# Blocks 2 and 3 of a two-layer feed-forward kernel: y by seven products after all of h, weight jobs at other ticks, some sums on GpSimd

## The chip, the cores and the metric

One core of a Trainium2 chip. The time is the device time of one execution in microseconds (us). A profiled execution also leaves a span, from its first to its last instruction, and a trace of every engine: PE (TensorE matmuls), PEld (TensorE weight loads), DVE (VectorE), ACT (ScalarE), POOL (GpSimd) and SP (SyncE, which here issues all DMAs, in order).

## The reference

Attention over chunks of 32 tokens, then two feed-forward layers, all in float32. 4 x 768 tokens, 8 heads of 64, so the layers see x of 3072 x 512; their hidden width is 2048.

```python
for c in range(nc):                       # 24 chunks of 32 tokens per sequence
    k_full = concat([mem_k, k[16 before .. 8 after the chunk]])   # 8 memory keys, windows of 56
    scores = scale * q_c @ k_full.T
    a = softmax(scores)                   # over 64 keys
    out[chunk] = a @ v_full
...
h = x @ w_in                              # first layer
g = np.maximum(h, 0.0) + np.log1p(np.exp(-np.abs(h)))     # softplus
x = g @ w_out
...
h = x @ w_in                              # second layer, other weights
g = h - np.tanh(h)
return g @ w_out
```

The weights and activations reach TensorE as pairs of a high part (rounded to the engine's float32r) and a low part (the rest), and each product is three matmuls: high x high, high x low, low x high.

## The kernel before

**Blocks.** The 3072 tokens are six blocks of 512 (N). In the first layer, block j takes 16 row blocks of h (f = 0 to 15), each 4 x 3 = 12 matmuls of 128x128 by 512 (`ff_h`), and for y 16 x 4 x 3 = 192 matmuls (`ff_y1`). Blocks 0 to 3 run f by f: h of f, softplus into t, gh and gl (the two parts) on ScalarE and VectorE, and two steps later (LAG) y of f. Blocks 4 and 5 are done as one block of 1024: first all h (384 matmuls; `act_g` puts softplus straight into the g tiles), then y by seven products of half-size matrices instead of eight (`y_phase`, 7 x 8 x 6 = 336 matmuls). The second layer does both h and y by seven products, for three blocks of 1024 (`h_phase`, `y_phase`).

**What seven products need.** The second factor of each product is a sum or difference of quarters. For the weights these are made on the chip: `job_w1(p)` (first layer, w_out), `job_w(kind, p)` (second layer, both matrices, which also converts float64 words to float32), each ending in `split_to`: hi on ScalarE, its store, lo on VectorE, its store, to DRAM (`wod`, `wid`). For x of the second layer `job_x` does so. For g, `y_steps` makes the differences (t2 and two sums in place) and, three steps ahead of TensorE (AHEAD), gh and gl of the next product; `gh` and `gl` have three tiles each. Weights for products come back from DRAM through a ring of slots (`Ring`), those of h of blocks 4 and 5 through `t_load` from `w1id`.

**The order.** Every engine's order is written out by hand. After an opening (block 0 and the first eight of 24 attention units), `tick()` is called once per twelve matmuls of 128x512 and places the other work of that moment: DMAs put off by `defer`, then the attention unit of the moment (128 tokens: scores `s_mm`, softmax, transposes `t_mm`, the copy pT `t_out`, `v_mm`, the two parts of x `x_out`), one unit every six ticks, then one step of each running job, then softplus, gh and gl of the f at hand. `JOBS` lists the ticks at which jobs begin; a job issues its load, waits four ticks (LEAD), and goes on by a step per tick. Ticks 0 to 95 are blocks 1 to 3, 96 to 129 the h stage of blocks 4 and 5 with the last y steps of block 3, 130 to 157 their y stage, then 56 per block of the second layer.

**Tiles that several users share.** `o` (four tiles of 4 KB per partition, handed out in turn) serves hi and lo of the jobs, the outputs of a block (`out1`) and of a y stage; the next user of a tile waits until its store has landed. `c2` is a job's scratch, `w15` its raw input (`w6`, `w5` for the four jobs in SECOND).

```python
def split_to(src, dst, shape):
    hi = opool.tile([P, *shape], F32R, name="o")
    nc.scalar.copy(out=hi, in_=src)
    yield
    put(hi, dst(0))
    lo = opool.tile([P, *shape], F32R, name="o")
    nc.vector.tensor_tensor(out=lo, in0=src, in1=hi.bitcast(F32), op=ALU.subtract)
    defer(put, lo, dst(1))
```

## Time and profile before

| | before |
|---|---|
| median of 3 runs | 1057.54 us (1057.13 to 1058.17) |
| profiled execution, its own time | 1057.51 us |
| its span | 1055.4 us |
| granted TensorE clock, mean | 0.997 |
| busy PE / PEld / DVE / ACT / POOL | 99 / 81 / 69 / 54 / 1% of the span |
| DMA moved | 303.19 MB, 287 GB/s mean |

Busy shares are of the span. Matmuls are pipelined and their ends are modelled, so one matmul's duration (390 ns) is longer than the time from one to the next. In rows of the timeline the columns are start (us), duration (us), engine, line, operation, output<-inputs, count, and in brackets how long the engine was idle before and for whom. In rows of groups they are busy us and mean ns of one, then idle time before.

### The profile page before, as it was taken

What the parts mean: (1) busy time and instruction counts of PE and PEld (TensorE: products, weight loads), DVE (VectorE), ACT (ScalarE), POOL (GpSimd) and SP (SyncE); (2) the same over time, 40 slices, a digit from 0 to 9 for tenths busy, and PEclk for the clock granted to TensorE, in tenths of its full rate; (3) what the DMA queues carried; (4) which work ended last, traced back from release to release, by engine and by line L of the source; (5) the groups of instructions that cost most, each with busy time, mean ns of one, the idle gap of its engine ahead of it and who ended that gap; (6) DMA issues with size and microseconds to landing.
All of it is one profiled execution on the core that took longest, in us unless ns stands there. A gap on an engine that the chain in (4) does not pass through costs nothing.

```text
span 1055.4 us, 18458 instructions
## 1 busy us (share of the span) xinstructions
PE 1044.2 (99%) x7368; PEld 857.4 (81%) x7370; DVE 727.6 (69%) x1129; ACT 567.1 (54%) x904; POOL 7.8 (1%) x14
## 2 busy tenths in 40 slices
PE   7999999999999999999999999999999999999998
PEld 5787888888888888888888888888888888888886
DVE  6998445845755657487677687777487877446876
ACT  6996454645656455354454555544455554344553
POOL 2000000000000000000000000000000000000000
PEclk8999999999999999999999999999999999999999
DMA  9989945857777986999987999978799788656651
GB/s 377 407 327 358 337 171 186 301 187 236 263 248 248 312 307 195 341 361 352 325 326 281 359 371 347 341 294 320 272 363 347 293 321 305 224 170 213 243 202 61
DMA packets 101269, 303.19 MB, mean 287 GB/s; under 512 B 8000, under 2 KB 55104, under 8 KB 83520
## 3 DMA queue, kind: packets, MB, share of 16 engines
q1 hardware_dynamic: 101184, 302.02, 79.5%
q8 instruction: 58, 0.95, 0.4%
q14 instruction: 27, 0.22, 0.1%
HBM read 211.29 MB, written 90.70 MB: 286 GB/s over the span
## 4 chain that ended last, share of the span: by engine, by line
PE 97%; DVE 1%; ACT 1%; DMA 0%; issue 0%; ACTq 0%
PE ps_y L387 47%; PE ps_h L387 32%; PE ps_b L387 13%; PE ps_a L361 2%; PE ps_a L280 1%; PE ps_a L332 1%; PE ps_h L880 1%; DMA qk<-in_qk 0%; PE ps_yy L361 0%; PE ps_h L399 0%; DVE gl L427 0%; DVE t L307 0%; DVE x L327 0%; ACT o L170 0%; PE ps_a L268 0%
## 5 line engine op out<-in xcount | busy, mean ns | idle before, releaser
L387 PE MATMUL ps_h<-x,w 128*128 128x512 f32 x900 | 215.3, 390 | 0.1
L704 ACT CAST gh<-w 128x512 fp32r<-128x512 f32 x224 | 139.0, 622 | 140.3 <-DVE gl L645 120.2
L645 DVE TENSOR_TENSOR gl<-w,gh 128x512 fp32r<-128x512 f32 x236 | 163.0, 691 | 71.4 <-ACT gh L704 64.9
L387 PEld LDWEIGHTS ps_h<-x,w 128*128 128x128 f32 x900 | 168.6, 188 | 35.4 <-ACT t L410 0.2
L387 PE MATMUL ps_y<-gh,w 128*128 128x512 f32 x512 | 172.9, 399 | 0.0
L387 PEld LDWEIGHTS ps_y<-gh,w 128*128 128x128 f32 x512 | 96.1, 188 | 21.3
L387 PE MATMUL ps_y<-gh,x 128*128 128x512 f32 x352 | 109.4, 389 | 0.0
L387 PE MATMUL ps_y<-gl,w 128*128 128x512 f32 x256 | 99.7, 390 | 0.0
L387 PE MATMUL ps_y<-w,x 128*128 128x512 f32 x402 | 94.5, 389 | 0.0
L387 PEld LDWEIGHTS ps_y<-w,x 128*128 128x128 f32 x402 | 75.5, 188 | 15.7
L427 DVE TENSOR_TENSOR gl<-t,gh 128x512 fp32r<-128x512 f32 x64 | 45.5, 713 | 55.8 <-ACT gh L422 55.6
L668 ACT ACTIVATE tanh<-sum 128x512 f32<-128x512 f32 x72 | 45.5, 632 | 60.0 <-DVE sum L641 59.8
L387 PEld LDWEIGHTS ps_y<-gh,x 128*128 128x128 f32 x352 | 66.1, 188 | 13.7
L410 ACT ACTIVATE t<-ps_h 128x512 f32<-128x512 f32 x64 | 38.1, 598 | 69.4 <-PE ps_h L387 65.8
L387 PE MATMUL ps_b<-gh,x 128*128 128x512 f32 x176 | 68.5, 389 | 0.0
L387 PE MATMUL ps_h<-gh,x 128*128 128x512 f32 x176 | 68.5, 389 | 0.0
L387 PE MATMUL ps_y<-gl,x 128*128 128x512 f32 x176 | 68.5, 389 | 0.0
L448 ACT CAST o<-c 128x1024 fp32r<-128x1024 f32 (+1 forms) x32 | 31.0, 969 | 69.6 <-DVE c L493 41.1
L645 DVE TENSOR_TENSOR w<-w 128x512 f32<-128x512 f32 x88 | 60.5, 688 | 6.8 <-ACT w L410 5.8
L387 PEld LDWEIGHTS ps_y<-gl,w 128*128 128x128 f32 x256 | 48.2, 188 | 9.0
L387 PE MATMUL ps_y<-x,w 128*128 128x512 f32 x240 | 55.2, 389 | 0.0
L387 PE MATMUL ps_b<-w,x 128*128 128x512 f32 x216 | 54.8, 389 | 0.0
(160 smaller groups left out, 1611.6 us busy)
## 6 DMA issues: line engine op xcount, KB each, us to landing
x<-wod SPq DMA_DIRECT2D x44, 1024.0 KB, 4.7
w<-x2d SPq DMA_DIRECT2D x21, 1024.0 KB, 6.8
x<-wid SPq DMA_DIRECT2D x21, 1024.0 KB, 6.1
wod<-o SPq DMA_DIRECT2D x32, 512.0 KB, 6.1
qk<-in_qk SPq DMA_DIRECT2D x21, 768.0 KB, 6.5
x2d<-o SPq DMA_DIRECT2D x30, 512.0 KB, 7.2
x<-wid SPq DMA_DIRECT2D x18, 768.0 KB, 6.8
ring<-wod SPq DMA_DIRECT2D x12, 1024.0 KB, 5.3
```

Of the source, the lines that this page charges most:

```text
L280: nc.tensor.matmul(out=ps[cc, j, KEYS * p : KEYS * (p + 1)], lhsT=a["q"][r, p, cc], rhs=a["k"][r, c, p, :], start=True, stop=True,)
L332: nc.tensor.transpose(ps[:, p * P : (p + 1) * P], a["sm"][:, p * P : (p + 1) * P], ident)
L361: nc.tensor.matmul(out=ps[h : h + 64, p % 2, 2 * P + t0 : 2 * P + t0 + CHUNK], lhsT=v, rhs=pT, start=True, stop=True,)
L387: nc.tensor.matmul(out=ps, lhsT=a, rhs=b, start=first and i == 0, stop=last and i == 2, skip_group_check=on,)
L410: nc.scalar.activation(out=out, in_=x, func=AF.Softplus)
L427: eng.tensor_tensor(out=gl, in0=t, in1=gh.bitcast(F32), op=ALU.subtract)
L448: nc.scalar.copy(out=hi, in_=src)
L645: nc.vector.tensor_tensor(out=out, in0=x, in1=y, op=ALU.subtract)
L668: nc.scalar.activation(out=t, in_=h, func=AF.Tanh)
L704: nc.scalar.copy(out=gh, in_=src)
L880: nc.tensor.matmul(out=ps_h[1], lhsT=zeros[:, :P], rhs=zeros, start=True, stop=True)
```

## The change

In blocks 2 and 3, which were two plain blocks, first all h is computed (`h_step`: f upward for block 2, downward for block 3, softplus into g tiles), then y of both by seven products (`y_phase(0, ...)`), as blocks 4 and 5 had it. Their w_in comes through `t_load` from `w1id` into w0 to w6 (`T1_LOADS`), the y weights through a ring of five of these slots. So w_out's sums (`job_w1`) must be ready by tick 66: all eight now begin at ticks 3 to 28, and their scratch c is an `o` tile. The t2 differences are made in the h stage, after each softplus of block 3 with f below 8. The attention units come at the ticks of `ATT_AT`, in plain order; x of units 20 to 22 no longer goes by way of DRAM (`x1d`); units 10, 11, 21 and 22 have their exponentials on ScalarE as eight instructions (`LATE_ACT`). Nine of the 16 w2 jobs (`BY_ACT`) convert with three ScalarE instructions and one of VectorE instead of one and three. Jobs whose sums fall into ticks 105 to 120 do these on GpSimd, and put the two halves of their sums through gh and gl tiles instead of o tiles. The x jobs of the first pair of blocks begin at ticks 86 and 94 (before: 42 and 54). Now ticks 0 to 31 are block 1, 32 to 65 h of blocks 2 and 3, 66 to 93 their y, 94 to 125 h of blocks 4 and 5, 126 to 153 their y; the second layer is as before.

```diff
-ATT_STEP = 6
-ATT_ORDER = (8, 9, 10, 11, 20, 12, 13, 14, 15, 21, 16, 17, 18, 19, 22, 23)
-VIA_DRAM = (20, 21, 22)
+ATT_AT = (0, 6, 14, 20, 28, 33, 38, 42, 46, 50, 54, 59, 64, 68, 74, 86, 92)
+ATT_FROM = 2 * UB
...
+T1_SLOT = (0, 4, 3, 2, 1, 5, 6, 0)
+T1_RING = (1, 2, 3, 4, 0)
+W1_ORDER = (7, 0, 4, 3, 2, 1, 5, 6)
 JOBS = (
-    (1, 15, 24, 43, 53, 76, 85, 94),
-    (5, 14, 23, 33, 66, 75, 84, 92, 95, 99, 102, 106, 109, 113, 117, 152),
-    (42, 54, 159, 169, 214, 224),
+    (3, 8, 4, 11, 18, 22, 25, 28, ),
+    (8, 15, 27, 37, 43, 49, 55, 89, 96, 99, 102, 105, 108, 111, 131, 148, ),
+    (86, 94, 156, 169, 206, 220, ),
 )
-SECOND = (95, 102, 109, 117)
-PHASES = ((1, NT - 1),) + tuple((2, b) for b in range(NT))
+SECOND = (89, 96, 102, 108, )
+BY_ACT = (8, 15, 27, 55, 99, 108, 111, 131, 148, )
+X_SLOT = (15, 7, 15, 15, 15, 15, )
+T1_LOADS = {9: 0, 13: 1, 17: 2, 21: 3, 25: 4, 29: 5, 33: 6, 38: 7, 54: 0}
+LATE_ACT = (10, 11, 21, 22, )
+T2_H = (105, 121)
+PHASES = ((1, 1), (1, 2)) + tuple((2, b) for b in range(NT))
...
+    def split_halves(src, dst):
+        for s in range(2):
+            ts = []
+            for i in (0, 2):
+                t = gpool.tile([P, 2, HALF], F32R, name="gl" if s else "gh")
+                if s:
+                    nc.vector.tensor_tensor(
+                        out=t, in0=src[:, i : i + 2], in1=his[i // 2].bitcast(F32), op=ALU.subtract
+                    )
+                else:
+                    nc.scalar.copy(out=t, in_=src[:, i : i + 2])
+                ts.append(t)
...
+        if by_act:
+            x = pool.tile([P, 4 * HALF, 2], U16, name=name, bufs=1)
+            nc.scalar.mul(x[:, :, 1].bitcast(F16), hi.bitcast(F32), SIGN_ONLY)
+            nc.scalar.activation(
+                out=x[:, :, 0], in_=lo, func=AF.Identity, scale=LOW_SCALE, bias=low_bias
+            )
+            nc.scalar.mul(hi.bitcast(F32), hi.bitcast(F32), EXP_BIAS)
+            yield
+            c = x.rearrange("p n two -> p (n two)").bitcast(U32)
             nc.vector.scalar_tensor_tensor(
-                out=c, in0=of, scalar=k, in1=c, op0=op, op1=ALU.bitwise_or
+                out=c, in0=hi, scalar=3, in1=c, op0=ALU.logical_shift_left, op1=ALU.bitwise_or
             )
...
-        sums(w)
-        yield
-        yield from split_to(w, lambda s: ((0, 4, place(s, 2, 4)),), [4, HALF])
-
-    def sums(w):
+        far = T2_H[0] <= now[0] < T2_H[1]
+        sums(w, nc.gpsimd if far else nc.vector)
+        yield
+        if far:
+            yield
+        if T2_H[0] <= now[0] < T2_H[1]:
+            yield from split_halves(w, lambda s, i: place(s, 2 + i, 2))
+        else:
+            yield from split_to(w, lambda s: ((0, 4, place(s, 2, 4)),), [4, HALF])
...
-        nc.vector.tensor_tensor(out=w[:, 2], in0=w[:, 2], in1=w[:, 1], op=sub)
-        nc.vector.tensor_tensor(out=w[:, 3], in0=w[:, 3], in1=w[:, 1], op=sub)
+        eng = eng or nc.vector
+        eng.tensor_tensor(out=w[:, 0], in0=w[:, 0], in1=w[:, 3], op=add)
+        eng.tensor_tensor(out=w[:, 1], in0=w[:, 0], in1=w[:, 1], op=sub)
+        eng.tensor_tensor(
+            out=w[:, 2:4], in0=w[:, 2:4], in1=w[:, 1:2].to_broadcast([P, 2, HALF]), op=sub
+        )
...
     def job_w1(p):
-        c = tpool.tile([P, 4, HALF], F32, name="c2", bufs=1)
+        c = opool.tile([P, 4, HALF], F32, name="o")
...
+                if not b and p % 4 == 3 and i * 2 + p // 4 >= 9:
+                    s = i * 2 + p // 4 - 9
+                    defer(t_load, s, s)
...
+        steps = [(0, f) for f in range(NF)] + [(1, f) for f in reversed(range(NF))]
+        prepared = []
+        t2 = []
+        prep = y_steps(prepared, t2)
+        ring = Ring((0,), ())
+        for n, (t, f) in enumerate(steps):
+            if t and f == NP - 1:
+                t2.extend(t2_tiles())
+            h_step(n, n == len(steps) - 1, t, f, x_tile(2 + t), t and f < NP and t2)
             if pend:
                 run_y()
                 tick()
+            if t and f % 2 == 0 and f < 2 * T_RING:
+                s = T1_RING[T_RING - 1 - f // 2]
+                defer(lambda s=s: ring.add(wpool.tile([P, 2048], F32R, name=f"w{s}")))
+        y_phase(0, prep, prepared)
```

`h_step` is the body of the old loop over h of blocks 4 and 5 (`ff_h`, then a tick with `act_g`), made a function; `act_g` gained one line:

```diff
+            if t2:
+                minus(t2[f // 4][:, f % 4], g2[f][:, 3], g)
```

## Rows read from the trace of the kernel before

**Rows 1.** The page: busy us of the engines, and the main DMA queue.
```profile
PE 1044.2 (99%) x7368; PEld 857.4 (81%) x7370; DVE 727.6 (69%) x1129; ACT 567.1 (54%) x904; POOL 7.8 (1%) x14
q1 hardware_dynamic: 101184, 302.02, 79.5%
```
**Rows 2.** Waits of PEld from 127 us on: total us, times, longest us.
```profile
PEld ps_a L361 <- issue: 4.6, 13, 0.4
```
**Rows 3.** The chain that ended last: start us, us, what.
```profile
670.75 76.16 PE ps_y L387 x336
```
**Rows 4.** Windows: length, busy us by engine (count), clock, DMA share, GB/s.
```profile
186.46:205.37 18.91, 18.91 (x205) 15.57 (x205) 17.31 (x30) 11.58 (x16) 0.00 (x0) 1.00 0.87 295
...
429.00:518.40 89.40, 89.40 (x396) 74.00 (x395) 61.60 (x86) 40.23 (x59) 0.00 (x0) 1.00 0.95 335
...
594.60:670.75 76.15, 76.15 (x337) 63.05 (x337) 59.35 (x94) 44.20 (x76) 0.00 (x0) 1.00 0.96 350
```
**Rows 5.** Groups by line and form: gl, softplus, pT.
```profile
L645 DVE TENSOR_TENSOR gl<-w,gh 128x512 fp32r<-128x512 f32 x236 | 163.0, 691 | 71.4 <-ACT gh L704 64.9
...
L410 ACT ACTIVATE t<-ps_h 128x512 f32<-128x512 f32 x64 | 38.1, 598 | 69.4 <-PE ps_h L387 65.8 <-DVE gl L427 2.9 <-PE ps_y L387 0.4
...
L344 ACT COPY pT<-ps_a 128x512 f32<-128x512 f32 x20 | 11.6, 582 | 3.9 <-PE ps_a L332 3.9
```
**Rows 6.** Timeline, ticks 1 to 6.
```profile
128.72 1.35 DVE L513 TENSOR_TENSOR c<-w 128x256 f32<-128x256 f32 x3
...
131.82 1.06 ACT L448 CAST o<-c 128x1024 fp32r<-128x1024 f32 x1 [2.63 <-DVE c L493]
...
135.95 3.69 SPq L788 DMA_DIRECT2D y1d<-o  x4
...
139.72 1.23 DVE L452 TENSOR_TENSOR o<-c,o 128x1024 fp32r<-128x1024 f32 x1 [0.42 <-DMA y1d<-o]
...
143.76 1.14 PE L361 MATMUL ps_a<-pT,v 64*64 64x32 f32 x64
```
**Rows 7.** DMA issues: count, KB each, median us to landing.
```profile
wod<-o SPq DMA_DIRECT2D x32, 512.0 KB, 6.1
...
y1d<-o SPq DMA_DIRECT2D x24, 256.0 KB, 7.1
```
**Rows 8.** Timeline after the scores of one unit.
```profile
145.72 0.59 ACT L375 CAST x<-ps_a 128x512 fp32r<-128x512 f32 x1 [0.60 <-PE ps_a L280]
...
146.34 0.69 DVE L307 TENSOR_REDUCE st<-ps_a 128x8 f32<-128x512 f32 x1 [4.79 <-ACT x L375]
...
147.67 0.68 DVE L377 TENSOR_TENSOR x<-ps_a,x 128x512 fp32r<-128x512 f32 x1
```
**Rows 9.** Timeline in the y stage of blocks 4 and 5.
```profile
551.11 0.62 ACT L704 CAST gh<-w 128x512 fp32r<-128x512 f32 x1 [0.74 <-DVE gl L645]
551.76 0.69 DVE L645 TENSOR_TENSOR gl<-w,gh 128x512 fp32r<-128x512 f32 x1
553.85 0.39 PE L387 MATMUL ps_b<-gl,x 128*128 128x512 f32 x1
```
**Rows 10.** Timeline: exponentials of one unit of the opening, first and last of 16.
```profile
84.33 1.28 ACT L316 ACT_TABLE_LOAD   x1
85.63 0.31 ACT L316 ACTIVATE sm<-ps_a,st 128x64 f32<-128x64 f32 x1
...
87.86 0.24 ACT L316 ACTIVATION_READ_ACCUMULATOR sm<-ps_a,st 128x1 f32 x1
```
**Rows 11.** Groups by line and form: GpSimd's subtractions in the opening.
```profile
L198 POOL TENSOR_TENSOR w<-o,w 128x1024 fp32r<-128x1024 f32 x1 | 2.4, 2399 | 72.5 <-ACT w L196 72.5
...
L198 POOL TENSOR_TENSOR w<-o,w 128x512 fp32r<-128x512 f32 x1 | 1.7, 1662 | 18.7 <-ACT w L196 18.7
```
**Rows 12.** Window in the h stage of blocks 4 and 5, columns as in rows 4.
```profile
450.00:490.00 40.00, 40.00 (x178) 33.10 (x178) 31.20 (x44) 18.23 (x27) 0.00 (x0) 1.00 1.01 356
```

More of the change, by code (lines that the diff above doesn't have):

```diff
@@ L1 @@
+from bisect import bisect_right
 from contextlib import ExitStack
@@ L75 @@
 SHARED = (7, 15)
-PLAIN = NB - 2
 T_LAG = 3
@@ L516, in job_w1, with job_x @@
         yield from split_to(c, lambda s: ((0, 4, wod[0][:, 2:6, p, s]),), [4, HALF])
-    def job_x(b, e, second=False):
-        raw = wpool.tile([P, 2, 2, N], F32, name="w6" if second else "w15")
+    def job_x(b, e, slot):
+        raw = wpool.tile([P, 2, 2, N], F32, name=f"w{slot}")
         nc.sync.dma_start(out=raw, in_=y1d[b][e])
@@ L693, in h_phase, with t2_tiles, y_steps @@
                 tick()
-    def y_steps(prepared):
-        t2 = [wpool.tile([P, 4, N], F32, name=f"w{i}") for i in (5, 6)]
-        sums_left = [(n, p) for n in range(3) for p in range(NP)]
+    def t2_tiles():
+        return [wpool.tile([P, 4, N], F32, name=f"w{i}") for i in (5, 6)]
+    def y_steps(prepared, t2=None):
+        sums_left = [(n, p) for n in range(0 if t2 is None else 1, 3) for p in range(NP)]
+        t2 = t2_tiles() if t2 is None else t2
         for q in PRODUCTS:
@@ L741, in y_phase @@
         for i, q in enumerate(PRODUCTS):
-            ps = [banks[(2 * b + d) % 4][i % 2] for d in range(2)]
+            ps = [(banks[2 * (b - 1) + d & 3] if b else ps_y[2 * d : 2 * d + 2])[i % 2] for d in range(2)]
             for p in range(NP):
@@ L800, in tick @@
                 run(soft.pop(u))
-        if r == 1 and before in VIA_DRAM:
-            run(soft.pop(("x", before)))
+        if k in T1_LOADS:
+            t_load(T1_LOADS[k], T1_SLOT[T1_LOADS[k]])
         active.extend(job() for job in plan.get(k, ()))
@@ L810, in tick @@
             s_mm(u, ps_a)
-        if r == 4 and u is not None:
+        t = min(4, ATT_AT[i + 1] - ATT_AT[i] - 1) if u is not None else -1
+        if r == t:
             t_mm(u, ps_a[:, 0, :])
         next(chain, None)
-        if r == 4 and u is not None:
+        if r == t:
             t_out(u)
@@ L959, in attention_ffn_ffn @@
             g = g2[f % NP][:, 2 * (f // NP) + t]
-            if n == len(steps) - 1:
-                prepared = []
-                prep = y_steps(prepared)
+            if last:
                 for _ in range(AHEAD):
                     next(prep)
-            tick(act_g(g, ps, g2[f][:, 0] if t and f < NP else None))
+            step()
+            tick(act_g(g, ps, g2[f][:, 0] if t and f < NP else None, f, t2))
+        steps = [(0, f) for f in range(NF)] + [(1, f) for f in reversed(range(NF))]
[7 more added lines that the diff above has]
+            h_step(n, n == len(steps) - 1, t, f, x_tile(2 + t), t and f < NP and t2)
             if pend:
@@ L968, in attention_ffn_ffn @@
                 tick()
[L969 to L975 removed]
+            if t and f % 2 == 0 and f < 2 * T_RING:
+                s = T1_RING[T_RING - 1 - f // 2]
+                defer(lambda s=s: ring.add(wpool.tile([P, 2048], F32R, name=f"w{s}")))
+        y_phase(0, prep, prepared)
+        steps = []
+        for f in range(NF + T_LAG):
+            steps += [(0, f)] * (f < NF) + [(1, f - T_LAG)] * (f >= T_LAG)
+        prepared = []
+        prep = y_steps(prepared)
+        for n, (t, f) in enumerate(steps):
+            x = x_tile(2 * (NT - 1) + t)
+            h_step(n, n == len(steps) - 1, t, f, x)
+            if now[0] > ATT_AT[-1] + 1 and lpool is None:
                 attention.close()
```

172 lines of the change are left out of this document (82 added, 90 removed).

## The prediction

> **What bounds the kernel now.** I read the profile from the engines inward. Shares first: TensorE is busy for 99% of the span; the DMA queue's packets take 79.5% of 16 engines [rows 1]. Then the waits of TensorE and of its weight loads from 127 us on, after the opening: for the matmuls the view lists none, for the loads gaps of at most 0.4 us [rows 2]. So from there the span is the sum of TensorE's work. Its rate: 336 matmuls in 76.16 us, 226.7 ns each [rows 3]; twelve of them, one tick of the planner, take 2.72 us. An edit pays if it takes matmuls away, and costs what it makes TensorE wait. The stages come last [rows 4]: the granted clock is 1.00, the 2.4 GHz level, in all of them; in the h stage of blocks 4 and 5 (429 to 518 us) VectorE works 61.6 of 89.4 us and DMA stands at 0.95, in the next h stage at 0.96.
>
> **The gain is a count.** Each of blocks 2 and 3 takes 192 matmuls for y; seven products take 7 x 8 x 6 = 336 for both. Their h stays at 384, the attention units stay at 16. 48 matmuls x 226.7 ns = **10.9 us**, four ticks: y of blocks 4 and 5 now begins with tick 126 instead of 130. All else is a question of waits. I walked the new order of instructions along TensorE's timeline with the durations of rows: gl 0.69, softplus 0.60, pT 0.58 us [rows 5].
>
> **Ticks 0 to 32 (block 1): eight w1 jobs and three w2 jobs.** A w1 job now takes its scratch c from the four o tiles. At tick 3 these hold the outputs of block 0, and c of the first job must wait until the first of them is stored: in before a lo of VectorE waited for the same release, to 139.72 us [rows 6]. c takes 3.1 us (128.72 to 131.82), so it is ready at 142.8. The planner puts hi of this job on ScalarE at tick 4, ahead of softplus and pT of unit 8: 1.06 + 0.60 + 0.58, less small overlaps, gives pT at 144.9. V of unit 8 wants it at 143.76 [rows 6]. A stall of **1.2 us**. The second job, a tick later, needs an o tile whose store has just gone out (median 6.1 us [rows 7]), so VectorE stands until 150 us; the softmax of unit 9 then ends near 156, its transposes are due at 158: covered by 2 us. Further on I find none in the block: a softplus result has 8 us until its bank is wanted. The w1id loads issued here have 10 to 20 ticks before use.
>
> **Ticks 32 to 66 (h of blocks 2 and 3).** The units come every four or five ticks. Between transposes and V of a unit lie 2.72 us; softplus and pT need 1.2, so 1 to 2 us are spare. At tick 35 hi of the w2 job begun at 27 takes an o tile that block 1's outputs have just filled, and waits for that store: 3.7 us (135.95 to the release [rows 6]) to 7.1 (the median [rows 7]). Softplus and pT of unit 13 stand behind: 0 to 1.7 us, I take **0.8**. Around tick 59 the job with three conversions on ScalarE and the differences t2 on VectorE push the job's sums until hi of tick 63 stands ahead of pT of unit 19: 0 to 1.4, I take **0.7**.
>
> **The step to y, tick 66.** Unit 20 is scored at tick 64, one h step before y begins. What follows a unit's scores (there they ended at 145.6): xh on ScalarE, then maximum, subtraction and xl on VectorE [rows 8]. After these stand two differences of the h step, and only then the first gl: 0.7 + 6 x 0.67 = 4.7 us after the scores, where the matmul that reads it is due at 2.72 + 0.23 = 2.95. A stall of 1.9 us; the last softplus, with a table load before the exponentials and one after, delays the softmax of unit 20 by some 0.4 more: **2.3 us**. Before, the step into a y stage had no attention unit and no differences beside it, since f ran upward there.
>
> **Ticks 66 to 94 (y of blocks 2 and 3).** The rhythm of a y stage: gh starts when its tile comes free (551.11), gl ends at 552.45, the matmul that wants it starts at 553.85 [rows 9]: 1.4 us of cover. Units 21 and 22 have their exponentials on ScalarE as eight instructions; such a group takes 2.5 us (85.63 to 88.10), after a table load of 1.28 [rows 10]. For unit 21 the table is softplus's and a kept copy (0.58) stands ahead: 0.6 + 1.3 + 2.5 = 4.4 us, of which 0.8 find ScalarE idle and 1.4 are cover. Stall **2.2 us**. For unit 22 no table load and no copy: **0.2**. VectorE has 53 gl, 16 differences, four units, seven outputs and part of an x job there, by the same rows some 67 of 86 us.
>
> **h of blocks 4 and 5, and after.** The sums of five w2 jobs go to GpSimd. Its nearest rows are 1.66 us for 512 columns and 2.40 for 1024 [rows 11]; from these I estimate 4.2 us for the three instructions of a job. They have two ticks, 5.4 us, before hi on ScalarE wants them, and softplus here runs over six banks: 13 us of lateness are covered. Price nothing; with that cover gone, up to 4.2 us per job, 21 in all. No gain either, as TensorE doesn't wait for VectorE there. The Trainium skill (SBUF — State Buffer, "Who interferes with whom") says that a VectorE instruction with two SBUF inputs and a GpSimd instruction that reads SBUF shut each other out for its whole length. By it each of the two engines would lose some microseconds per job, which the same 13 us swallow; the rows read here do not show both side by side.
>
> The jobs that only move keep their instructions. New DMA work: 14 loads of y weights and nine more of w1id, 1 MB each, less four of w1d and 3 MB through x1d: 17 MB on 302 [rows 1]. Where it bunches is rival 2.
>
> **Sum.** The profiled execution took 1057.51 us, 2.1 more than its span and 0.03 under the median of the runs. 1057.5 - 10.9 + (1.2 + 0.8 + 0.7 + 2.3 + 2.2 + 0.2 = 7.4) = **1054.0 us**, 0.33% faster. Less than 0.2% (2.1 us) a measurement of this kernel hardly tells from no change; "faster" ends at 1055.4, "slower" begins at 1059.6.
>
> **Rivals.** 1. *All hidden.* Each stall rests on the order within one tick, and where TensorE stands once, later waits shrink; up to all 7.4 us may vanish: 1046.6 us. For it: no wait in 900 us of before, although VectorE worked 17.3 of 18.9 us around one unit [rows 4]. Against it: there the cover was several us, in the places above 1.4 or less. Chance of 1050 or less: 0.18.
>
> 2. *DMA comes late in the h stage of blocks 4 and 5: the slower side.* In ticks 94 to 122 the plan issues six w2 jobs (2.9 MB each, loads and stores), the stores of a seventh, 6.8 MB of the two x jobs that ran at ticks 42 and 54, and the weights: 31.7 MB in 76 us, 416 GB/s, where I count 25 MB in before. With DMA at 1.01, 40 us moved 356 GB/s [rows 12]. By tick 113 the plan has issued 26.9 MB and 19.4 can have moved: 7.5 MB behind, 21 us. The w1id loads issued at ticks 101, 105 and 109 are wanted ten ticks, 27 us, later. SP issues in order; if the stores ahead hold it up by 6 us on top of the queue, each further us is one of TensorE, and with 5 to 8 of them the time is 1059 to 1062. Against it: tiles that aren't free hold the jobs back, which thins the queue. Chance 0.20. The Trainium skill (DMA: Bandwidth & Descriptors, the measured table from HBM to SBUF) gives 425 GB/s for a core alone with 16 MB. By that the stretch would keep up and this rival would be nearly out; the 40 us of [rows 12] lie lower, and they decide.
>
> 3. *More lumps reach TensorE.* The x job begun at tick 86 puts 2 us lumps on VectorE at 1.4 us of cover; the jobs at ticks 22 to 25 wait for stores issued one tick earlier, and if those take 10 us instead of 6, pT of unit 12 (0.4 us spare in my walk) is late. 2 to 5 us more: 1056 to 1059. Chance 0.14.
>
> **How the numbers follow.** Forecast as summed (1050 to 1055.4) 0.48, rival 1 0.18, rival 2 0.20 (0.13 slower, 0.06 within the bound, 0.01 faster), rival 3 0.14 (0.10 within, 0.04 slower). Faster 0.67, same 0.16, slower 0.17. The range 1047 to 1061 leaves out rival 1 with everything hidden and the far end of rival 2; the likeliest case alone has 1050 to 1055.4.
>
> **What the profile after should show.** Some 48 matmuls fewer. Waits of TensorE on pT of unit 8 (1.2 us), on gl at the first y step of blocks 2 and 3 (1.9), and on gh or gl behind the first group of exponentials there (2.2): each that is absent takes its term out of the sum. DMA near 1.0 in the h stage of blocks 4 and 5, w1id loads landing after up to 20 us, without a wait of TensorE; a wait on such a load is rival 2. A y stage of blocks 2 and 3 much over 91 us (28 ticks, four units at 18.91 - 6 x 2.72 = 2.6 us, and 4.7 of stalls) is rival 3. I am wrong altogether if the matmuls run above 226.7 ns or TensorE waits in stages that the change leaves alone.

## The result and the profile after

The changed kernel takes 1069.85 us (median of 4 runs, 1067.13 to 1073.44). The ratio to the kernel before is 1.0121, with a 95% interval of 1.0088 to 1.0155: some 12.5 us slower than the 1057.34 of the kernel before in the same measurement. The forecast was 1054.0 us, the range ended at 1061, and slower had a chance of 0.17. The profiled execution took 1067.13 us with a span of 1065.0, so 9.6 us more than before's; all the accounts below are made against these two. It is the shortest of the four, so what makes the median 2.7 us longer is in no profile.

The page after has the count that the forecast began with, and 17 MB more in the queue. Engines first (busy us, share, instructions), then the DMA queue (packets, MB, share), then the shares of the chain that ended last:

```profile
PE 1037.8 (97%) x7322; PEld 846.1 (79%) x7322; DVE 738.9 (69%) x1132; ACT 607.2 (57%) x1010; POOL 23.3 (2%) x29
q1 hardware_dynamic: 100784, 318.80, 82.9%
PE 81%; DMA 7%; DVE 5%; ACT 5%; issue 2%; SPq 0%; ACTq 0%; DVEq 0%
```

Against [rows 1] there are 46 matmul records fewer where 48 matmuls were taken out. But TensorE's share fell from 99% to 97%, and its share of the chain, 97% before, is 81%, with 7% of DMA and 5% each of VectorE and ScalarE. The waits of TensorE's matmuls from 127 us on, a view that had no row before (engine, line, waited for: us in total, times, longest):

```profile
PE ps_h L384 <- ACT w L407: 3.6, 2, 2.9
PE ps_y L384 <- ACT w L407: 2.8, 2, 2.0
PE ps_a L338 <- DVE sm L333: 2.6, 2, 1.9
PE ps_y L384 <- ACT gh L752: 1.8, 2, 1.4
PE ps_y L384 <- issue: 1.1, 1, 1.1
PE ps_b L384 <- ACT gh L752: 0.7, 1, 0.7
...
```

The first two rows are waits for softplus (L407), all four in the h stage of blocks 4 and 5, where the forecast held it covered. The stages show where. Three windows of after, columns as in [rows 4]: y of blocks 2 and 3, h of blocks 4 and 5, y of blocks 4 and 5:

```profile
336.94:426.49 89.55, 87.20 (x802) 70.05 (x801) 63.88 (x108) 50.32 (x108) 0.00 (x0) 1.00 0.67 244
426.49:524.26 97.77, 91.37 (x385) 74.09 (x384) 55.67 (x70) 52.60 (x78) 15.35 (x15) 0.97 0.99 346
524.26:602.71 78.45, 77.26 (x338) 62.83 (x337) 59.09 (x91) 44.65 (x68) 0.00 (x0) 1.00 0.97 364
```

The h stage has 384 matmuls, which take 384 x 0.2267 = 87.05 us. It took 97.77: **10.7 us are lost in this one stage**, where the forecast has a price of nothing. Inside it the DMA queue stands at 0.99, and it moved 346 GB/s x 97.77 us = 33.8 MB. Two things make up the loss. One is stalls. Here is the first, on ScalarE, and below it a longer wait that cost TensorE nothing (start us, us, instruction, idle before and releaser):

```profile
431.52 0.61 ACT L574 CAST o<-w 128x512 fp32r<-128x512 f32 x1
436.35 0.83 ACT L466 CAST o<-w 128x768 fp32r<-128x768 f32 x1 [4.23 <-DMA y1d<-o]
437.09 1.08 ACT L407 ACTIVATE w<-ps_h 128x512 f32<-128x512 f32 x2
445.67 1.05 ACT L466 CAST o<-w 128x1024 fp32r<-128x1024 f32 x1 [7.51 <-DMA x2d<-o]
```

L466 is hi of the w2 job begun at tick 89. It wants one of the four o tiles, and these hold outputs of the y stage whose stores are still under way. ScalarE's order is fixed by the program, so two softplus stand behind it; the first four h steps use only two banks for their results (ps_h), and TensorE stands until the banks are read. The wait that ends at 445.67 falls into the steps with six banks, and no matmul starts late by 0.3 us or more from 442 us until 495:

```profile
433.74 1.07 PE L384 MATMUL ps_h<-x,w 128*128 128x512 f32 x4
437.73 4.59 PE L384 MATMUL ps_h<-x,w 128*128 128x512 f32 x12 [2.92 <-ACT w L407]
442.16 4.01 PE L384 MATMUL ps_y<-x,w 128*128 128x512 f32 x17
```

The second thing is the clock. Twelve matmuls took 4.59 us after the stall, 17 took 4.01 a little later. The windows say why: behind the wait the granted clock is 0.53, near the 1.2 GHz level, then 0.99, the 2.4 GHz level again. The last row shows the same behind the stall of 2.1 us at 496:

```profile
437.70:441.30 3.60, 3.57 (x9) 2.79 (x10) 0.00 (x0) 0.47 (x1) 0.00 (x0) 0.53 1.00 411
441.30:444.90 3.60, 3.60 (x18) 2.98 (x17) 1.93 (x4) 0.00 (x0) 0.00 (x0) 0.99 1.07 370
495.50:499.30 3.80, 3.33 (x8) 2.66 (x9) 1.56 (x2) 2.46 (x3) 0.98 (x2) 0.56 1.01 305
```

So the stage's 10.7 us are 3.1 + 2.1 + 1.0 + 0.8 = 7.0 of stalls (437, 496, 501, 511 us); of the other 3.7, 3.4 are the slow matmuls after the first two, 1.7 each. ScalarE's waits for stores in the stage, then those in the h stage before the change:

```profile
ACT gh L453 <- DMA wod<-gh: 11.2, 3, 5.9
ACT o L466 <- DMA x2d<-o: 10.2, 2, 7.5
...
ACT o L466 <- DMA y1d<-o: 4.2, 1, 4.2
```

```profile
ACT o L448 <- DMA wod<-o: 7.1, 2, 4.8
ACT o L448 <- DMA y1d<-o: 5.9, 1, 5.9
```

So ScalarE waited for stores before the change too, 13.0 us in all, and TensorE did not wait once. Now it is 25.6 us, and ScalarE has more work beside them: 52.60 us of 97.77, where [rows 4] has 40.23 of 89.4.

And the DMA view of the same stretch (issues, KB each, median us to landing): the stores, and the loads that the forecast feared:

```profile
w<-w1id SPq DMA_DIRECT2D x4, 1024.0 KB, 8.4
...
wod<-gh SPq DMA_DIRECT2D x10, 256.0 KB, 7.6
...
x2d<-gh SPq DMA_DIRECT2D x5, 256.0 KB, 9.4
...
y1d<-o SPq DMA_DIRECT2D x2, 256.0 KB, 10.3
```

Stores of 256 KB land after 7.6 to 10.3 us (medians). In the same stage before, where the queue stood at 0.95, they took 6.7 and 7.0:

```profile
wod<-o SPq DMA_DIRECT2D x14, 256.0 KB, 6.7
...
y1d<-o SPq DMA_DIRECT2D x4, 256.0 KB, 7.0
```

So the stores land some 1 to 3 us later than before, and ScalarE waits for them six times instead of three. The w1id loads land after 8.4 us and nothing waits for them.

### The profile page after: what moved, and what is told of

Its sections match the earlier page's. It is cut to its first block, busy times and chain, and to the rows that moved or that the text cites. A ratio compares the mean times of both kernels' runs of the same rounds, so it can differ in the third digit from the quotient of the medians.

```text
span 1065.0 us, 18607 instructions
## 1 busy us (share of the span) xinstructions
PE 1037.8 (97%) x7322; PEld 846.1 (79%) x7322; DVE 738.9 (69%) x1132; ACT 607.2 (57%) x1010; POOL 23.3 (2%) x29
## 4 chain that ended last, share of the span: by engine, by line
PE 81%; DMA 7%; DVE 5%; ACT 5%; issue 2%; SPq 0%; ACTq 0%; DVEq 0%
PE ps_y L384 44%; PE ps_h L384 21%; PE ps_b L384 12%; PE ps_a L367 2%; DMA wod<-gl 2%; DMA x2d<-o 1%; PE ps_a L286 1%; DMA ring<-wod 1%; DMA w<-in_w1o 1%; DVE w L690 1%; DVE gl L690 1%; DMA w<-in_qk 1%; PE ps_a L338 1%; DMA wid<-o 1%; ACT w L407 1%
## 5 line engine op out<-in xcount | busy, mean ns | idle before, releaser
L752 ACT CAST gh<-w 128x512 fp32r<-128x512 f32 x280 | 173.6, 624 | 169.8 <-DVE gl L690 125.1
L690 DVE TENSOR_TENSOR gl<-w,gh 128x512 fp32r<-128x512 f32 x298 | 204.7, 690 | 91.9 <-ACT gh L752 84.9
L384 PE MATMUL ps_h<-x,w 128*128 128x512 f32 x660 | 160.2, 395 | 4.0 <-ACT w L407 3.6
L384 PE MATMUL ps_y<-gh,w 128*128 128x512 f32 x480 | 157.7, 396 | 1.4 <-ACT gh L752 1.4
L384 PEld LDWEIGHTS ps_h<-x,w 128*128 128x128 f32 x660 | 124.0, 189 | 31.8 <-ACT w L407 4.4
L384 PE MATMUL ps_y<-x,w 128*128 128x512 f32 x480 | 115.3, 396 | 3.9 <-ACT w L407 2.8
L384 PEld LDWEIGHTS ps_y<-x,w 128*128 128x128 f32 x480 | 90.5, 190 | 24.3 <-ACT w L407 3.7
L384 PE MATMUL ps_y<-w,x 128*128 128x512 f32 x402 | 94.5, 389 | 0.0
L690 DVE TENSOR_TENSOR w<-w 128x512 f32<-128x512 f32 x104 | 71.6, 689 | 21.1 <-ACT w L407 19.8
L690 DVE TENSOR_TENSOR w<-w,w 128x512 f32<-128x512 f32 x80 | 54.9, 686 | 0.0
L686 DVE TENSOR_TENSOR sum<-ps_y,kept 128x512 f32<-128x512 f32 x36 | 24.9, 692 | 43.1 <-PE ps_y L384 36.0
L384 PEld LDWEIGHTS ps_y<-gl,w 128*128 128x128 f32 x240 | 45.1, 188 | 10.4 <-DVE gl L690 1.7
```

The costliest lines, as they stand in the source:

```text
L384: nc.tensor.matmul(out=ps, lhsT=a, rhs=b, start=first and i == 0, stop=last and i == 2, skip_group_check=on,)
L686: nc.vector.tensor_tensor(out=h, in0=ps, in1=t, op=ALU.add)
L690: nc.vector.tensor_tensor(out=out, in0=x, in1=y, op=ALU.subtract)
L752: nc.scalar.copy(out=gh, in_=src)
```

## The experiments

Theory A: the queue is full in the h stage of blocks 4 and 5, stores of scratch tiles land late, ScalarE waits in order for a tile, and softplus stands behind it. Theory B: the sums on GpSimd are the harm, through VectorE or by coming late. From e5 on B2 takes its place: the harm is the order of ScalarE's own work, whatever the queue does. The lumps of the y stages are a separate question. The measure for A and B is the length of the h stage, 87.04 us where nothing stalls, beside its traffic (GB/s times length). Each run's own profile, one execution, gave these; the times are medians, those of the kernel before 1057.2 to 1058.6 on the chips used.

```
run                       h of 4,5 us   MB    y of 2,3   y of 4,5   time us  ratio to before (95%)
the changed kernel          97.77      33.8     89.55      78.45    1069.85  1.0088 to 1.0155
e1  short stores, copies    90.25      21.3    103.42      78.44    1071.84  1.0096 to 1.0144
e2  sums on VectorE        100.44      34.6     90.81      78.44    1073.42  1.0122 to 1.0164
e3  more tiles              94.10      33.9     91.04      78.43    1067.90  1.0061 to 1.0127
e4  lumps of y              98.35      33.9     89.30      77.91    1066.91  1.0063 to 1.0101
e5  short stores            91.99      24.2     91.45      78.41    1062.80  1.0031 to 1.0072
e6  x jobs early            87.04      27.2    102.88      78.41    1072.04  1.0107 to 1.0165
e7  e6, jobs spaced         98.48      26.2    102.70      78.47    1081.51  1.0206 to 1.0271
e8  e7, y edits             96.29      26.2    106.10      76.88    1083.83  1.0228 to 1.0280
e9  softplus first          94.90      33.4     89.68      78.44    1064.56  1.0037 to 1.0091
e10 y order                 98.02      34.1     90.80      76.87    1064.31  1.0037 to 1.0084
e11 e9 and e10              92.91      32.9     90.79      76.91    1059.72  1.0004 to 1.0029
e12 e11, jobs at 30 to 44   93.32      33.0     90.70      76.92    1060.43  1.0015 to 1.0038
e13 e11, more tiles         93.40      33.4     90.73      76.87    1057.64  0.9989 to 1.0018
e14 e13, sums on VectorE    90.55      33.3     90.74      76.89    1058.00  0.9995 to 1.0023
e15 e13, x early, GpSimd    87.04      27.2    104.03      76.87    1066.78  1.0071 to 1.0097
e16 e14, five jobs there    87.04      30.3     90.71      84.14    1062.45  1.0025 to 1.0059
e17 e16, jobs at 30 to 44   90.90      30.5     90.76      83.75    1062.14  1.0022 to 1.0048
```

**Is it the traffic, or GpSimd? (e1, e2, e5, e6)**

e1 stores a sliver of each product and fills the places beforehand by copies inside the DRAM; e5 does without the copies and reads other products in their place.

```diff
# e5 (e1: the slice in put() for ticks 95 to 124, and seven copies of wid[0])
-            return wid[p][:, a : a + n, s] if kind == "i" else wod[1][:, a : a + n, p, s]
+            if kind == "i":
+                return wid[p][:, a : a + n, s]
+            return wod[1][:, a : a + n, p, s, : 16 if p < 6 else HALF]
...
-            nc.sync.dma_start(out=place, in_=t[:, at : at + n].bitcast(F32))
+            nc.sync.dma_start(out=place, in_=t[:, at : at + n, : place.shape[-1]].bitcast(F32))
```

> What it leaves out: from tick 95 to 124 the w2 jobs store only 16 of 256 columns of each product, so some 12 MB less go through the DMA queue in the h stage of blocks 4 and 5; seven copies inside the DRAM fill those places beforehand, in ticks 68 to 86, and the second layer then reads other numbers. Every instruction of TensorE, ScalarE, VectorE and GpSimd stays. Theory A (the queue is full in that stage, the stores of scratch tiles land late, ScalarE stands in order behind them and softplus behind ScalarE, then TensorE runs at half clock for some us): the 10.5 us lost there fall below 2.5, the time to 1058 to 1062. Theory B (the sums on GpSimd hinder VectorE and come late to ScalarE): they stay, 1066 to 1071.

> The run with short stores again, without its copies: the six w2 jobs begun at ticks 96 to 111 store 16 of 256 columns of each product, some 10 MB less in the h stage of blocks 4 and 5; the second layer reads the products of the other two jobs in their place (as many bytes), so its y is another. Engines' work unchanged. Theory A (the queue is full, scratch tiles come free late): the waits after 450 us (2.1 + 1.9 at half clock + 1.0 + 0.8 = 5.8 us) go, the first one at 437 (3.1 and 1.7) stays, since nothing is shortened before it: 1063 to 1066. Theory B2 (what stalls is the order of ScalarE's work itself, three conversions of a job in one tick and two jobs at a time): they stay, 1067 to 1072.

The time of e1 missed both ranges. Its copies did harm of their own (e5, without them, has 91.45 us in the y stage where e1 has 103.42): there ScalarE's copy for an x job waited 11.3 us for a load (the profile names a w2 job's), a gh stood behind it, and TensorE waited 9.6 us, the same kind of chain in another stage:

```profile
ACT o L575 <- DMA w<-in_w2i: 11.3, 1, 11.3
...
PE ps_y L384 <- ACT gh L753: 9.6, 1, 9.6
```

Past 455 us, where the stores are short, the stage had no stall. e5 shows it without that damage. Its windows, up to 450 us and from there to the stage's end:

```profile
428.91:450.00 21.09, 18.04 (x73) 14.47 (x72) 10.36 (x15) 8.48 (x12) 0.00 (x0) 0.92 1.02 359
450.00:520.90 70.90, 70.90 (x315) 58.72 (x313) 45.55 (x55) 44.13 (x66) 14.90 (x15) 1.00 0.74 235
```

The first stall, with nothing shortened ahead of it, is still there (3.2 us, and slow matmuls after it); then TensorE is busy for 70.90 of 70.90 us, with all of GpSimd's work (14.90 us) and ScalarE's order unchanged in that window. That speaks against B and B2 alike. 1062.8 us is just under the range that A gave, 1063 to 1066.

```diff
# e2
-T2_H = (105, 121)
+T2_H = (0, 0)
# e6
-    (86, 94, 156, 169, 206, 220, ),
+    (61, 74, 156, 169, 206, 220, ),
-X_SLOT = (15, 7, 15, 15, 15, 15, )
+X_SLOT = (15, 15, 15, 15, 15, 15, )
```

> Undoes one part: the sums of the five w2 jobs back on VectorE, and their second halves through o tiles again. Theory A (late stores): what ScalarE waits for in the stage becomes o tiles alone, which are as late; the loss of 10.5 us stays within 3 us, 1065 to 1072. Theory B (GpSimd): only the wait at the stage's begin stays (3.1 us and some 1.7 at half clock), 5 to 6 us come back, 1061 to 1065.

> One part moved: the two x jobs of blocks 0 and 1 begin at ticks 61 and 74 instead of 86 and 94, so their 9 MB leave the h stage of blocks 4 and 5 and the end of the y stage before it. Theory A: the y outputs of blocks 2 and 3 are stored sooner, the wait at 437 goes (4.8 us), and of the later ones half; VectorE's lumps in the y stage of blocks 2 and 3 cost 1 to 2 us more: 1061 to 1066. Theory B2 (order of ScalarE's work): at most the wait at 437 changes, the lumps are added, 1067 to 1072.

With the sums back on VectorE the stage lost 13.4 us instead of 10.7, and e2 (1073.42 us, 1.4 above A's range) is no faster than the changed kernel: theory B falls. (B2's sum for e6, 1067 to 1072, comes near the time, but not by its reasons.) In e6 the sums stayed on GpSimd, and with the x jobs gone the stage had no stall at all, the first one included. Their traffic left together with their work (VectorE 43.07 us in the stage instead of 55.67, ScalarE 47.44 instead of 52.60), so e6 alone doesn't tell one from the other; e5, which takes away bytes alone, does. e6's windows, y of blocks 2 and 3, then h of blocks 4 and 5:

```profile
336.30:439.18 102.88, 92.47 (x801) 70.09 (x800) 73.89 (x126) 55.59 (x117) 0.00 (x0) 0.98 0.81 282
439.18:526.22 87.04, 87.04 (x385) 72.09 (x384) 43.07 (x52) 47.44 (x67) 14.91 (x15) 1.00 0.90 312
```

But the time missed A's range: the y stage gave up 13.3 us (102.88 against 89.55) to the two jobs, where I had taken 1 to 2. I take it that its cover of 1.4 us per product [rows 9] has no room for an x job's pairs of differences; no run shows that by itself.

**Tiles, spacing and order (e3, e7, e9)**

e3 has four more tiles for the jobs of that stage, in space that is first used in the y stage after it. e7 is e6 with the w2 jobs every four ticks (`SECOND` and `BY_ACT`, which name jobs by their ticks, follow). e9 moves one call.

```diff
# e3
-        hi = opool.tile([P, *shape], F32R, name="o")
+        pool, name = (opool, "o") if extra is None else (extra, "o2")
+        hi = pool.tile([P, *shape], F32R, name=name)
...
+                extra = more.enter_context(tc.tile_pool(name="m", bufs=4, reuse_waits="tile"))
# e7, beside e6's edit
-    (8, 15, 27, 37, 43, 49, 55, 89, 96, 99, 102, 105, 108, 111, 131, 148, ),
+    (8, 15, 27, 37, 43, 49, 55, 86, 90, 94, 98, 102, 106, 110, 131, 148, ),
# e9
+        if 94 <= k < 126:
+            next(chain, None)
         active.extend(job() for job in plan.get(k, ()))
...
-        next(chain, None)
+        if not 94 <= k < 126:
+            next(chain, None)
```

> Four more scratch tiles for the w2 jobs alone in the h stage of blocks 4 and 5 (in the space of tiles that are first used in the y stage after it), also for the second halves; the sums stay on GpSimd, the DMA traffic is the same. Theory A (late stores hold ScalarE): the job begun at tick 89 no longer waits for the outputs of blocks 2 and 3, the others find free tiles: 7 to 9 of the 10.5 us go, 1059 to 1063; if the queue itself is the limit and only the place of the wait changes, less than 3 go. Theory B (GpSimd): nothing changes there, 1066 to 1071.

> As the run before, and the w2 jobs of that stage begin every four ticks from 86 on (86, 90, 94, 98, 102, 106, 110) instead of 89, 96, 99, 102, 105, 108, 111. Theory A: the DMA share in the stage falls under 0.95 and its loss under 2 us of 10.5; the lumps outside it stay: 1058 to 1062. Theory B2: spacing helps by 2 to 3 us, 1065 to 1068.

> All traffic stays; only the order of ScalarE within a tick changes: from tick 94 to 125 the softplus of the h step is issued ahead of the jobs' conversions and copies instead of behind them. Theory A in its narrow form (a copy that waits for a scratch tile's store does harm because softplus stands behind it): a waiting copy now has one tick, 2.7 us, more until it delays a softplus that TensorE wants, so the 3.1, 2.1, 1.0 and 0.8 us fall to 1 us together and the 3.6 us at half clock go: 1060 to 1063. Rival: the tiles come so late that ScalarE's waits of 4 to 6 us reach the next softplus all the same, less than 4 us come back, 1066 to 1070.

e3: the first stall is gone, and 3.7 us come back in the stage, about half of what A expected of tiles. Its time, 1067.90, lies in B's range and not in A's; but B had said that nothing would change in the stage. ScalarE's waits for the stores of the new tiles are as long as those for gh (6.4 us at most, against 5.9); the row stands here, and it says that the queue is late, not only that tiles are few:

```profile
ACT o L467 <- DMA wod<-o: 16.9, 4, 6.4
```

e7 was a miss for both theories: 11.4 us lost at 266 GB/s. Nearly all of it is one wait of ScalarE for an o tile's store, 9.1 us, which made TensorE wait 8.5 us at 452, and the slow matmuls after it. The stage's mean hides a bunch: the jobs now begun at 86, 90 and 94, the y outputs and the w1id loads meet where the h stage begins. Two windows:

```profile
440.00:460.00 20.00, 11.69 (x39) 9.05 (x39) 8.10 (x11) 5.88 (x7) 0.00 (x0) 0.74 0.97 336
460.00:480.00 20.00, 20.00 (x90) 16.58 (x89) 8.93 (x12) 11.23 (x14) 0.00 (x0) 1.00 0.70 247
```

So it is not the stage's bytes that count but those around the wait. That the place with two banks is the worst for them fits the stalls at 437 and 452, but was not tried by itself.

e9 is the plainest trial of the mechanism: no byte and no instruction less, only softplus ahead of the copies. The stage fell from 97.77 to 94.90 us, the first stall vanished, and the median fell by 5.3 us to 1064.56, between the two ranges (A had said 1060 to 1063, the rival 1066 to 1070). Of the 4.5 us between the two profiled executions 2.9 lie in this stage; 1.3 lie ahead of it, where the edit changes nothing, and are scatter. The stalls at 494 and 499 us stayed (3.3 and 2.5 us): there ScalarE's waits for gh's stores, 6.1 us the longest, reach past the tick that was won.

**The lumps of the y stages (e4, e8, e10)**

```diff
# e4
-ATT_AT = (... 59, 64, 68, 74, 86, 92)      LATE_ACT = (10, 11, 21, 22, )
+ATT_AT = (... 59, 63, 68, 74, 86, 92)      LATE_ACT = (10, 11, )
-BY_ACT = (8, 15, 27, 55, 99, 108, 111, 131, 148, )
+BY_ACT = (8, 15, 27, 55, 99, 108, 111, )
# e10: e4, but ATT_AT = (... 59, 68, 74, 80, 86, 92), and in job_w's conversion on VectorE
+                if now[0] > 126 and of is hi:
+                    yield
# e8: e7, LATE_ACT and BY_ACT as in e4 (units 21, 22 and jobs 131, 148 out), e10's yield, and ATT_AT = (... 54, 58, 62, 68, 74, 86, 92)
```

> Three small edits outside that stage: unit 20 a tick earlier (63 instead of 64), exponentials of units 21 and 22 as one instruction with the subtraction and the sum on VectorE, and the conversion of the w2 jobs begun at ticks 131 and 148 as three VectorE instructions instead of three on ScalarE. If my terms are right (step to y 2.1 us, unit 21 2.1, the job's three instructions ahead of gh in the y stage of blocks 4 and 5 1.8), each place falls below 0.7 and the time by 4 to 5 us, to 1064 to 1066. Rival: the lumps only change engine, ScalarE's for VectorE's, less than 1.5 us come back, 1068 to 1070.

> As the run before, and against the lumps in the y stages: units 19 and 20 at ticks 58 and 62 instead of 59 and 64, units 21 and 22 with one exponential instruction, and the conversion of the jobs begun at ticks 131 and 148 on VectorE, in two ticks. If the terms are as I read them (2.1 + 2.1 + 1.8 us), 4 us less than the run before, 1054 to 1058; if lumps only change place, less than 2 us less.

> The lumps of the y stages alone: units 20 to 23 at ticks 68, 74, 80 and 86 instead of 64, 68, 74 and 86, so none is scored just before the step to y; one exponential instruction for units 21 and 22; the conversion of the jobs begun at ticks 131 and 148 on VectorE in two ticks. The step's 2.1 us and the first lump of y (2.1) fall to 1.2 together, the 1.8 us in the y stage of blocks 4 and 5 to 0.5: 1065 to 1067. If lumps only change place: 1068 to 1071.

In e4, whose time of 1066.91 lies between its two ranges, the exponentials of unit 21 cost 0.7 us instead of 2.1, as one instruction of 0.63 us in place of eight. The step to y did not get cheaper (0.3 + 1.3, 0.7 some 5 us later, and 0.6 for an earlier unit), nor much the y stage of blocks 4 and 5 (1.05 instead of 1.36: the conversion's two VectorE instructions of 2.5 us stand ahead of gl in place of ScalarE's ahead of gh). e10 has the better answer for both: unit 20 scored two ticks into y leaves 1.4 us at the step, and the conversion cut in two leaves 0.4 in the later y stage (76.87 us, before 76.16). The time fell to 1064.31, a little under its range. e8, built on e7, inherits its stall; units 19 and 20 at 58 and 62 cost 3.3 us at unit 19's transposes, and the step to y 3.5. It had been forecast at 1054 to 1058 and is the slowest of all.

**Together, and what then bounds it (e11 to e17)**

e11 is e9 with e10; e12 moves the jobs of ticks 27, 37 and 43 to 30, 38 and 44; e13 is e11 with e3's tiles, e14 that with e2's edit. e15 is e13 with e6's edit and the x jobs' differences on GpSimd (`eng = nc.vector if b else nc.gpsimd`), through o tiles alone. e16 and e17 are e14 and its variant with the jobs as in e12, with five w2 jobs in the stage instead of six, and other jobs in `SECOND` and `BY_ACT` (the three jobs of the y stage convert on VectorE):

```diff
-    (8, 15, 27, 37, 43, 49, 55, 89, 96, 99, 102, 105, 108, 111, 131, 148, ),
+    (8, 15, 27, 37, 43, 49, 55, 89, 96, 100, 104, 108, 112, 124, 135, 146, ),
```

> The two runs before this one together. If the losses are independent: 9 + 4 us less than the changed kernel, 1055 to 1058. If a delay taken away in one place comes back at the next wait: 1060 to 1065.

> As the run before, and the w2 jobs begun at ticks 27, 37 and 43 begin at 30, 38 and 44, so that no store of a job's halves holds the o tiles when block 1's outputs are copied out: the wait of unit 13's transposes (2.1 us) goes, 1054 to 1057; if the later job's halves then stand behind the outputs' stores in their turn, as I had forecast for ScalarE, no gain: within 1 us of the run before.

> The run with both orders (softplus first in the h stage of blocks 4 and 5; units and jobs of the y stages moved), and in addition the four more scratch tiles of that h stage for both halves of its w2 jobs, so that no half goes through gh and gl. What is left there is 1.7 + 2.6 + 1.2 us behind copies that wait for gh's stores. If these waits are a matter of tiles, they fall under 1.5 us together: 1055 to 1057.5. If the queue is what is late (the extra tiles alone left 6.6 of 10.5 us), they only move: 1058.5 to 1061.

> As the run before with the sums of the five jobs on VectorE. Once no wait for tiles covers it, this prices the GpSimd part alone. Theory A: within 1.5 us of the run before, on either side. Theory B (GpSimd's sums, longer and in a tick of their own, are a loss): 2 to 4 us faster than it.

> The tiles run with the first two x jobs at ticks 61 and 74 and their differences on GpSimd, all through o tiles. The 9 MB leave the h stage (whose stalls then were nil) and VectorE has none of the 22 differences that made 11 us of stalls in the y stage of blocks 2 and 3 when the jobs were moved there. If VectorE's lumps were the cause there: stage after stage near what the counts say plus 3 to 5 us, 1049 to 1054. If ScalarE's conversions of these jobs ahead of gh, or VectorE slowed beside GpSimd, do the same: 1056 to 1064.

> The tiles run with the sums on VectorE, and five w2 jobs instead of six between ticks 96 and 122, begun every four ticks (96, 100, 104, 108, 112); the other three go to the y stage of blocks 4 and 5 (124, 135, 146). If the queue's lateness is what is left in the h stage (3 us), it falls under 1 us, and each job in the y stage costs at most the 0.45 us seen there: 1053 to 1056.5, faster than the kernel before. If a job in that y stage costs as much as the stage gains, 1057 to 1060.

> As the run before, with the w2 jobs of ticks 27, 37 and 43 at 30, 38 and 44: the wait of unit 13's transposes (1 to 2 us) goes and some 0.4 us come in at 275 us: 0.5 to 1.5 us less than the run before; a rival is no difference, the profiled waits there vary by as much from one execution to the next.

e11 comes to 1059.72: of the 9 and 4 us hoped for, 5.3 and 5.5 came one by one and 10.1 together, so the parts nearly add; e9's was far below the 9 hoped for, and 1059.72 lies between the two ranges given. e12 takes the wait of unit 13 away (2.1 us in the changed kernel, none now) without a gain in the median: its profile has a new wait of 1.6 us at 274.7 us, in the midst of a unit's scores, and the twelve matmuls behind it take 4.43 us. e17, with the same jobs moved, has it too (1.5 us); e11 and e16 have not. Its cause was not followed. e13 and e14 reach the kernel before, 1057.64 and 1058.00, and do not beat it. e13 lies just above the range for tiles (1055 to 1057.5), but in its profile the waits for stores only moved: 18.9 us for the new tiles, and 6.4 us lost in the stage. Their stages, first e13's, then e14's:

```profile
428.07:521.47 93.40, 89.38 (x386) 72.90 (x384) 55.13 (x65) 52.51 (x73) 16.19 (x15) 0.98 0.99 358
423.17:513.72 90.55, 87.79 (x386) 71.84 (x384) 59.15 (x80) 52.19 (x73) 0.00 (x0) 1.00 1.00 368
```

The queue is busy throughout both (0.99 and 1.00), with 33.4 and 33.3 MB, where TensorE needs 87 us. What a busy queue moves differs from stage to stage: 358 and 368 GB/s here, 379 in the y stages that follow in both runs, 385 in e11's. At 379 the bytes would take 88 us, at 385 just under 87, so that bytes alone bound the stage is near, but not shown. The difference between the two stages is not shown to be GpSimd's: these are single executions, e13's a long one (1062.27) and e14's its shortest (1054.63). The medians are 0.4 us apart, less than either's interval of some 1.5 us to each side, so no cost of the sums on either engine is seen.

e16 takes one job out. The stage is at 87.04 us, 3.5 less than e14's, and the y stage after it pays 7.3, 84.14 against 76.89. The time, 1062.45, is above both of its ranges (the worse one ended at 1060):

```profile
424.46:511.50 87.04, 87.04 (x386) 72.07 (x384) 54.41 (x74) 47.24 (x68) 0.00 (x0) 1.00 0.96 348
511.50:595.64 84.14, 79.62 (x337) 63.66 (x336) 68.63 (x104) 43.03 (x68) 0.00 (x0) 0.98 0.97 371
```

e17 has nearly the same y stage (83.75), in the h stage a stall of 2.1 us that e16's profile lacks, and the same time: no gain from moving the job of unit 13. In e15 the h stage is at 87.04 again, and the y stage of blocks 2 and 3 at 104.03 although VectorE has none of the jobs' differences; 1066.78 is above both of its ranges. TensorE waited for gl there (first row), hardly for ScalarE's gh (0.4 us). The gl themselves took longer (second row e15 from 337 to 424 us, then the changed kernel in the same stretch):

```profile
PE ps_y L384 <- DVE gl L697: 9.5, 7, 2.4
L697 DVE TENSOR_TENSOR gl<-w,gh 128x512 fp32r<-128x512 f32 x48 | 42.9, 906 | 8.9 <-ACT gh L759 8.6
L690 DVE TENSOR_TENSOR gl<-w,gh 128x512 fp32r<-128x512 f32 x55 | 37.5, 689 | 21.0 <-ACT gh L752 19.9
```

With GpSimd's differences in the same stage gl takes 906 ns on average instead of 689, 10.4 us more for 48 of them. Of the two rivals written down for e15 that points to the slower VectorE, not to ScalarE's conversions.

## Why the prediction was wrong

**The step that failed** is in the part on h of blocks 4 and 5: "softplus here runs over six banks: 13 us of lateness are covered. Price nothing". It cost 10.7 us. The cover was worked out for the sums on GpSimd, which indeed cost nothing that a run shows (e6, e15: none lost with them in place; e14 against e13); they took 3.1 us per job (15.35 us for five), less than the 4.2 estimated. But it was used as a price for the whole stage, and it has two holes. The first four h steps alternate between two banks, as the code says, so that the cover there is one tick: 4.2 us of waiting cost 3.1. And later a late copy doesn't come late alone: ScalarE's softplus are queued behind it, so its waits for tiles (11.2 + 10.2 + 4.2 us here) and the jobs' conversions between them add up against the same 13 us. A single wait may still be covered, as the 7.51 us at 445.67 were, and the 13.0 us of them in the same stage before the change.

**The rival that came nearest** had the right crowd and the wrong door. Rival 2 counted 31.7 MB in 76 us (28 ticks) against 356 GB/s; the whole stage (32 ticks) moved 33.8 MB in 97.77. It let the lateness reach TensorE through the w1id loads, which had 27 us; they landed after 8.4. And it held that "tiles that aren't free hold the jobs back, which thins the queue": they hold ScalarE back. The stores of o, gh and gl hold tiles with no slack, and that is where it came in (e5, e9). With the door right, [rows 12] would have done: 31.7 MB at 356 GB/s take 89 us, 13 more than the 76 that TensorE had for these ticks. It was given 0.20 and 5 to 8 us instead.

**The Trainium skill** was weighed at this place. The Trainium skill (DMA: Bandwidth & Descriptors, the measured table from HBM to SBUF) has 425 GB/s for 16 MB. The h and y stages of blocks 4 and 5 in these runs with the queue at 0.96 or more show 344 to 385 GB/s, so the 356 of [rows 12] was the better choice and rival 2 not nearly out. The Trainium skill (DMA: Bandwidth & Descriptors, Where 436 GB/s comes from) also has about 358 GB/s as the share of the HBM for a core, which the forecast did not weigh. The traces lie on both sides of that figure and nearer to it than to 425; an estimate by it is 94.5 us for the stage's 33.8 MB, against 97.77 measured. For the price of the sums the forecast named the Trainium skill (SBUF — State Buffer, "Who interferes with whom"), by which a VectorE instruction with two SBUF inputs and a GpSimd instruction that reads SBUF contend. The trace of e15 agrees: gl took 906 ns for 689.

Point by point, from the gaps between matmul starts in the profiled execution:

```
place                                forecast   measured us
48 matmuls fewer                       -10.9      -10.9
pT of unit 8 (tick 6)                    1.2        0
hi behind block 1's outputs (unit 13)    0.8        2.1, at unit 13's softmax, on VectorE
pT of unit 19                            0.7        0.3
step to y                                2.3        2.1 (1.26 + 0.87)
exponentials of unit 21                  2.2        2.1
unit 22                                  0.2        0.2
h of blocks 4 and 5                      0         10.7
y of blocks 4 and 5                      0          2.3 (78.45 - 76.16)
y of the second layer's first blocks     0          1.3 (77.46 - 76.16)
sum                                     -3.5      +10.2
```

The profiles differ by 9.6 us; the other 0.6 were not followed up.

**The lumps** of ticks 0 to 94 sum to 6.8 us against 7.4, most of them at the place named. That the sums agree so well is partly luck: unit 8's 1.2 us too many stand against unit 13's 1.3 too few. Unit 8's is absent, since the outputs of block 0 were stored in time. The one at unit 13 had the right cause, a store that holds an o tile, and the wrong engine. VectorE's copy of block 1's output waits for a w2 job's store, and the softmax of unit 13 stands behind it:

```profile
238.43 0.69 DVE L438 COPY o<-ps_y 128x512 f32<-128x512 f32 x1 [4.90 <-DMA wid<-o]
...
240.19 0.69 DVE L333 TENSOR_TENSOR sm<-sm,st 128x512 f32<-128x512 f32 x1
```

The terms for the step to y and unit 21 were of the right size (for gl at the step, the prediction's own 4.7 - 2.95 is 1.8 and not the 1.9 that it says); e4 and e10, which changed their causes, moved them. Not seen at all were the job begun at tick 131 in the y stage of blocks 4 and 5 (1.8 of the 2.3 us there, 1.4 of them behind three conversions on ScalarE ahead of gh; e10 brings that stage from 78.45 to 76.87) and 1.3 us in the next y stage, which every run kept and whose cause I did not try.

**What stays open.** From one execution to the next e13 varies from 1054.4 to 1062.5 us. Each run has one profile, so whether the stalls of the h stage come and go with that is not shown; e16's and e17's profiles, with the same jobs in that stage, differ there by 3.9 us. Which stores come late in which execution was not followed.

## What to carry to other kernels

When an engine works in order, ask of each instruction that takes a scratch tile whose store frees that tile, and what stands behind it: here the lateness of a full queue entered there, and the prefetched loads were never late. Issuing the urgent instruction first (e9) took no extra instruction or byte. Add up the bytes of a stage and divide by the rate that the trace shows with the queue full; if that exceeds the matmuls' time, expect the queue to set the stage's length. Moving work only helps if another stage has both room in the queue and engine time to spare (in e6 and e16 the stage that took the work paid more than the other gained). Price each stage for all that the change puts there, not for its most conspicuous part.

## What the hardware showed unasked

After the stalls of 3.1 and 2.1 us at 437 and 496 us TensorE's granted clock was 0.53 and 0.56 for the next 3.6 and 3.8 us, near the 1.2 GHz level, which added some 1.7 us to each; after those of 1.0 and 0.8 us, and after one of 2.1 us at 241, it stayed at 1.00. The length of the stall alone does not say which it will be: in e9 the clock stayed at 1.00 over the 3.6 us after a stall of 3.3 us, and in e5 it was 0.62 after one of 1.6. The first row is e9's, the second e5's:

```profile
493.90:497.50 3.60, 3.02 (x12) 2.18 (x12) 2.16 (x3) 2.38 (x2) 1.32 (x2) 1.00 0.94 314
357.90:361.50 3.60, 3.38 (x8) 2.51 (x9) 3.53 (x8) 1.92 (x4) 0.00 (x0) 0.62 0.48 197
```

The sums on GpSimd slow VectorE by nearly as much as they overlap it, in the one case read here. In e3 a pair of VectorE instructions took 3.46 us, where the same pair without GpSimd beside it takes 2.48 (the job begun at tick 89 in the changed kernel: 2.49); first VectorE, then GpSimd:

```profile
480.44 3.46 DVE L504 SCALAR_TENSOR_TENSOR w<-w,w 128x1024 uint32<-128x1024 uint32 x2
479.94 1.62 POOL L531 TENSOR_TENSOR c<-c 128x512 f32<-128x512 f32 x1
```

The two overlap by 1.12 us, and the pair is 0.98 longer.
